# The order of the first two chunks written anew in a windowed-attention and feed-forward kernel

## The chip, the cores and the metric

The kernel runs on one core of a Trainium2 chip. The metric is the device time of one execution in microseconds (us); of several runs the median counts.

## What is computed

For 8 batches and 8 heads of 64 elements there are 512 local and 32 global tokens. A global token attends to all 544 tokens; a local one to the 32 global tokens and to the local tokens within 32 places. The heads are joined to rows of 512 elements, and each row then goes through a norm and a two-layer feed-forward network with a residual:

```python
s_ll = where(abs(pos[:, None] - pos[None, :]) <= 32, scale * q_l @ k_l.T, -1e9)
s_lg = scale * q_l @ k_g.T
out_l = sm(concat([s_lg, s_ll])) @ concat([v_g, v_l])
out_g = sm(scale * q_g @ k_all.T) @ v_all
x = join_heads(concat([out_g, out_l]))
xn = (x - mean(x)) / sqrt(var(x) + 1e-6) * g_ln
out = x + maximum(xn @ w_ch1, 0) @ w_ch2      # 512 -> 2048 -> 512
```

All of it is float32. A float32 product with enough precision is made of several products of high and low halves: a tile is split into a high part (a rounded copy) and a low part (what the rounding left).

## The kernel before, in words

The rows of x are worked in chunks of 512, one batch's local rows each, and a last one for the global rows. Chunk 0 needs its attention before its feed-forward part can start, and the weights have to be loaded, joined and split into halves while that part already runs. From chunk 1 on all weights lie ready in SBUF.

*Attention of chunk 0* comes in 8 units: 4 pairs of heads (0 to 3) times 2 halves of 256 rows. The numbers of units in this text, 0 to 7, are in the order of the program. A unit's steps, with engine and line of the kernel before:

- load of its tile `u` (queries, keys and values; SyncE, `dma`, L405); `score`, 32 small products per unit into two banks (TensorE, L542); `lowest`, four times, the mask with the row's minimum (VectorE, L554); `exp`, four times (ScalarE, L566)
- `turn`, four transposes `tp<-ident,p` (TensorE, L578); `turned`, their copy to SBUF (ScalarE, L583); `sums`, 32 small products `pv<-u,pt` (TensorE, L597); `total` (GpSimd, L609) and `inverse` (VectorE, L612) of the exponentials' sums; `scale`, the product of the two into x (VectorE, L616)
- the sums of a unit wait for the scaling of the unit before, and its `total` for the scaling three units before.

The *norm* of a half is `stats` (VectorE, L468, once for each pair of heads and 128 rows), `join` (L471), `widen` (L474), `root` (GpSimd, L478), `shift` (VectorE, L481), and `apply`, on ScalarE (L487) or VectorE (L493). Then `turn_x` transposes x (TensorE, L798) and `high_x` and `low_x` split it (ScalarE L812, VectorE L816).

The *weights* come in 16 pieces f of 128 hidden columns, each in two parts of 512 columns: load `raw<-in_wd` (L405), `bound`, a clamp (VectorE, L434), `size` and `third`, two conversions (ScalarE, L441 and L444), `place`, a merge of bits (VectorE, L447), `high` (ScalarE, L453) and `low` (VectorE, L456).

The *feed-forward part* takes for each f three groups of four products, high by high, high by low and low by high (`first`, L838, `ph<-xh,w`); `hh`, relu and rounding (ScalarE, L847); `hl`, the low half of the hidden tile (VectorE, L861); and four groups of three products (`second`, L873, `acc<-w,hh`). The `second` products of f stand behind the `first` ones of f+1.

Between them stand the *visits*: the attention of the next chunk's units, two units at a time, of tiles `u_e` (queries and keys) and `u_v` (values) that are loaded apart (L522 and L524). A visit makes the scores of the pair that comes next and the sums of the pair before (L542, L597). The loads for a later visit wait until the visit before has read the tiles.

Nothing is emitted where the code for it stands. `begin_plan` and its helpers build some 3000 numbered operations with `Plan.op`, each with an engine, the operations that it needs and a function that emits its instructions. `Plan.emit` then takes for each engine the operations in the order of the numbers in `ORDER` until that list is used up, and by key and reckoned time after that. `WARM` gives the number of warm-up products (L983, `none<-ident`, results used by nobody) that are put ahead of the TensorE operation with that number; where an operation isn't named there and the planner reckons with idle time ahead of it in the start, it puts in as many as fill that time:

```python
idle = max(free[e], AWAKE)
fill = int((t - idle - MARGIN) / spare) if t < FULL else 0
for _ in range(WARM.get(o.number, fill)):
    words += 2 * self.spare(idle)
```

SyncE issues the loads of the first chunks in the order of its list too, and waits at each until its tile is free. The lists cover the five engines to the end of the program; on TensorE the operations 17 to 191 are those of chunk 0's attention and norm, 625 to 793 the feed-forward part of chunk 0, with chunk 1's attention 422 to 621 in between.

Of the kernel before, what the change touches and what calls it, by code (L numbers as in the profile page):

```python
# [74 lines left out]
WARM = {19: 4, 28: 1, 53: 3, 102: 7, 170: 1, 625: 6}  # L75
# [11 lines left out]
        19 36 53 28 45 70 108 30 62 125 79 47 142 64 117 81 159 134 151 119 168 136 153 170 96-97 102-103  # L87
        184-186 191 625-627 422 630-632 635-641 644-650 653-658 445 659 662 433 663-664 451 665-668 671-677 474
        462 680-682 482 683-686 689-694 505 493 695 698 524 699-704 707-713 547 716-717 535 718-719 555 720-722
        725-731 734-740 743-749 752-758 781 761 784 787 762-764 790 765-768 1051-1053 793 1056-1058 1061-1067  # L90
        1070-1076 1079-1082 852 1083-1085 1088-1094 1097-1103 1106-1111 922 1112 1115-1121 1124-1130 1133-1139
        981 1142-1148 1151-1157 1160-1166 1169-1175 1178-1184 1187-1194 1537-1539 1279 1542-1544 1547-1553
        1556-1562 1565-1569 1338 1570-1571 1574-1580 1583-1589 1592-1597 1408 1598 1601-1607 1610-1616 1619-1625
        1467 1628-1634 1637-1643 1646-1652 1655-1661 1664-1670 1673-1680 2023-2025 1765 2028-2030 2033-2039
        2042-2048 2051-2055 1824 2056-2057 2060-2066 2069-2075 2078-2083 1894 2084 2087-2093 2096-2102 2105-2111
        1953 2114-2120 2123-2129 2132-2138 2141-2147 2150-2156 2159-2166 2509-2511 2251 2514-2516 2519-2525
        2528-2534 2537-2541 2310 2542-2543 2546-2552 2555-2561 2564-2569 2380 2570 2573-2579 2582-2588 2591-2597
        2439 2600-2606 2609-2615 2618-2624 2627-2633 2636-2642 2645-2652 2995-2997 2737 3000-3002 3005-3011
# [12 lines left out]
        403 617 568 592 619 397 408 618 521 414 593 399 742 594 569 411 595 620 596 413 570-571 622 572-573 751  # L111
        417 597 405 598 574 419 599-600 575 783 601 576 786 760 602 565 577-580 603-604 789 605 792 606-607 581
        591 775 779 773 1055 794 796 820 777 798 800 822 824 826 804 830 805 1060 806 831-834 807-811 835-837
        812 1069 838-839 813 840-841 814-816 851 842-844 817 803 818 850 829 819 1078 845 853 879 855 881 857
        883 909-910 859 885 913-914 862 915-916 863 1087 917 888-889 864 890 865 919 891 866 892 867 893 868 894
        869 895 870 896 1096 871 897 872 898 873 899 874 900 875 901 876 902 877 903 878 904 1207-1208 1105
        1209-1221 923 949 925 951 927 953 979-980 929 955 1222-1223 1114 933 932 959 958 934 960 935 961 936 962
        937 963 938 964 939 965 940 966 941 1123 967 942 968 943 969 944 970 945 971 946 972 947 973 948 974
        1224-1225 1132 1226-1238 1141 982 1008 984 1010 986 1038-1039 1012 988 1014 1042-1043 991 1044-1045 992
        1046 1017-1018 993 1019 994 1048 1020 995 1021 996 1022 997 1150 1023 998 1024 999 1025 1000 1026 1001  # L120
        1027 1002 1028 1003 1029 1004 1030 1005 1031 1239 1159 1240-1254 1168 1255-1270 1177 1006 1032 1007 1033
        1186 1272 1274 1276 1278 1199 1201 1203 1205 1541 1280 1306 1336-1337 1282 1308 1284 1310 1286 1312 1546
        1290-1291 1289 1315-1316 1292 1317 1293 1318 1294 1319 1295 1320 1296 1321 1297 1555 1322 1298 1323 1299
        1324 1300 1325 1301 1326 1302 1327 1303 1328 1304 1329 1305 1564 1330-1331 1339 1365 1395-1396 1341 1367
        1343 1369 1345 1371 1573 1399-1403 1348-1349 1374-1375 1350 1376 1405 1351 1377 1352 1378 1353 1582 1379
        1354 1380 1355 1381 1356 1382 1357 1383 1358 1384 1359 1385 1360 1386 1361 1591 1387 1362 1388 1363 1389
        1364 1390 1693-1703 1409 1435 1465-1466 1411 1437 1600 1413 1439 1415 1441 1704-1707 1419 1418 1445 1444
        1420 1446 1421 1447 1422 1448 1609 1423 1449 1424 1450 1425 1451 1426 1452 1427 1453 1428 1454 1429 1455
        1430 1618 1456 1431 1457 1432 1458 1433 1459 1434 1460 1708-1714 1627 1715-1724 1468 1494 1524-1525 1470
        1496 1472 1498 1474 1500 1528-1530 1636 1531-1532 1477-1478 1503-1504 1479 1505 1534 1480 1506 1481 1507  # L130
        1482 1508 1483 1509 1484 1510 1645 1485 1511 1486 1512 1487 1513 1488 1514 1489 1515 1490 1516 1491 1517
        1725-1726 1654 1727-1742 1663 1743-1756 1492 1672 1518 1493 1519 1758 1760 1762 1764 1685 1687 1689 1691
        2027 1766 1792 1822-1823 1768 1794 1770 1796 1772 1798 2032 1776-1777 1775 1801-1802 1778 1803 1779 1804
        1780 1805 1781 1806 1782 1807 1783 2041 1808 1784 1809 1785 1810 1786 1811 1787 1812 1788 1813 1789 1814
        1790 1815 1791 2050 1816-1817 1825 1851 1881-1882 1827 1853 1829 1855 1831 1857 2059 1885-1889 1834-1835
        1860-1861 1836 1862 1891 1837 1863 1838 1864 1839 2068 1865 1840 1866 1841 1867 1842 1868 1843 1869 1844
        1870 1845 1871 1846 1872 1847 2077 1873 1848 1874 1849 1875 1850 1876 2179-2189 1895 1921 1951-1952 1897
        1923 2086 1899 1925 1901 1927 2190-2193 1905 1904 1931 1930 1906 1932 1907 1933 1908 1934 2095 1909 1935
        1910 1936 1911 1937 1912 1938 1913 1939 1914 1940 1915 1941 1916 2104 1942 1917 1943 1918 1944 1919 1945
        1920 1946 2194-2200 2113 2201-2210 1954 1980 2010-2011 1956 1982 1958 1984 1960 1986 2014-2016 2122  # L140
        2017-2018 1963-1964 1989-1990 1965 1991 2020 1966 1992 1967 1993 1968 1994 1969 1995 1970 1996 2131 1971
        1997 1972 1998 1973 1999 1974 2000 1975 2001 1976 2002 1977 2003 2211-2212 2140 2213-2228 2149 2229-2242
        1978 2158 2004 1979 2005 2244 2246 2248 2250 2171 2173 2175 2177 2513 2252 2278 2308-2309 2254 2280 2256
        2282 2258 2284 2518 2262-2263 2261 2287-2288 2264 2289 2265 2290 2266 2291 2267 2292 2268 2293 2269 2527
        2294 2270 2295 2271 2296 2272 2297 2273 2298 2274 2299 2275 2300 2276 2301 2277 2536 2302-2303 2311 2337
        2367-2368 2313 2339 2315 2341 2317 2343 2545 2371-2375 2320-2321 2346-2347 2322 2348 2377 2323 2349 2324
        2350 2325 2554 2351 2326 2352 2327 2353 2328 2354 2329 2355 2330 2356 2331 2357 2332 2358 2333 2563 2359
        2334 2360 2335 2361 2336 2362 2665-2675 2381 2407 2437-2438 2383 2409 2572 2385 2411 2387 2413 2676-2679
        2391 2390 2417 2416 2392 2418 2393 2419 2394 2420 2581 2395 2421 2396 2422 2397 2423 2398 2424 2399 2425
        2400 2426 2401 2427 2402 2590 2428 2403 2429 2404 2430 2405 2431 2406 2432 2680-2686 2599 2687-2696 2440  # L150
# [1458 lines left out]
```

## Time and profile before

| | before |
|---|---|
| median of 3 runs | 882.84 us (881.62 to 883.41) |
| profiled execution | 883.14 us |
| its span in the trace | 881.3 us |
| TensorE products (PE) busy | 866.5 us, 98% of the span |
| VectorE (DVE) busy | 696.1 us, 79% |
| ScalarE (ACT) busy | 316.1 us, 36% |
| GpSimd (POOL) busy | 68.1 us, 8% |
| mean granted TensorE clock | 0.995 of full speed |

The table is of one execution. Busy time is the sum of an engine's instructions, and PEld, where it stands in a row, is TensorE's loading of weights, which runs beside its products. DMA is the mean busy share of the core's 16 DMA engines. A share over the whole span is a mean over stages with different limits: what bounds a stage is read from that stretch alone. "Idle before" behind a row of the order of time is the engine's idle time ahead of it, with the instruction that ended last before; the name is inferred.

### The profile page before, as it was taken

The numbers are of one execution on the slowest core, as the hardware profiler recorded it, in microseconds if no ns is written. First come the engines' busy times: TensorE is split into PE (matmuls) and PEld (weight loads), VectorE is DVE, ScalarE is ACT, GpSimd is POOL, SyncE is SP. The second block draws the span as 40 slices with busy tenths as digits, with TensorE's granted clock in tenths as the row PEclk, the third lists the DMA queues.
The fourth block names the chain that finished last, engine by engine and source line by source line (L and its number), as shares of the span: only waits on it lengthen the run. The fifth ranks groups of instructions, "written<-read, shape, count | busy, mean of one in ns | idle before, by whom it ended". The sixth has DMA issues, their size and how long they took to land.

```text
span 881.3 us, 21518 instructions
## 1 busy us (share of the span) xinstructions
PE 866.5 (98%) x8489; PEld 703.8 (80%) x8489; DVE 696.1 (79%) x2501; ACT 316.1 (36%) x895; POOL 68.1 (8%) x162
## 2 busy tenths in 40 slices
PE   7899999999999999999999999999999999999997
PEld 4588778888888888888888888888888788787897
DVE  4878688899778998799879997889879888787311
ACT  7788874223123223223223222223323222233211
POOL 4100000000000000000000000000000112222000
PEclk9999999999999999999999999999999999999999
DMA  9778835424124323324233403333331536355100
GB/s 345 295 245 279 283 100 184 157 82 152 43 87 134 115 87 129 105 80 152 81 106 126 152 0 128 104 104 128 128 105 48 204 130 221 121 195 198 65 21 24
DMA packets 42869, 119.88 MB, mean 136 GB/s; under 512 B 5136, under 2 KB 6160, under 8 KB 41744
## 3 DMA queue, kind: packets, MB, share of 16 engines
q1 hardware_dynamic: 42576, 118.25, 38.8%
q8 instruction: 66, 1.08, 0.5%
q14 instruction: 35, 0.29, 0.1%
q10 hardware_dynamic: 192, 0.26, 0.1%
HBM read 100.67 MB, written 17.83 MB: 134 GB/s over the span
## 4 chain that ended last, share of the span: by engine, by line
PE 93%; DVE 2%; DMA 2%; ACT 2%; issue 1%; POOL 1%; SPq 0%; ACTq 0%; POOLq 0%; DVEq 0%
PE ph L838 41%; PE acc L873 41%; PE sc L542 4%; PE pv L597 3%; PE pv L747 1%; PE sc L659 1%; DMA u_e<-in_eq 1%; ACT p L566 1%; DMA raw<-in_wd 1%; PE tp L578 1%; PE none L983 1%; PE t L798 1%; DVE w L456 0%; DVE tmp L447 0%; DVE p L554 0%
## 5 line engine op out<-in xcount | busy, mean ns | idle before, releaser
L873 PE MATMUL acc<-w,hh 128*128 128x512 f32 x1088 | 335.7, 390 | 0.0
L838 PE MATMUL ph<-xh,w 128*128 128x512 f32 (+1 forms) x1216 | 302.1, 375 | 1.1 <-DVE hl L861 1.0
L838 PEld LDWEIGHTS ph<-xh,w 128*128 128x128 f32 x1216 | 215.6, 188 | 43.8 <-DVE hl L861 1.7
L873 PEld LDWEIGHTS acc<-w,hh 128*128 128x128 f32 x1088 | 204.5, 188 | 41.4
L847 ACT ACTIVATE hh<-ph 128x512 fp32r<-128x512 f32 (+1 forms) x144 | 82.5, 573 | 415.2 <-PE ph L838 415.2
L589 DVE STREAM_TRANSPOSE pt<-p 32x128 f32<-32x128 f32 x768 | 207.2, 289 | 10.0 <-ACT p L566 1.6
L873 PE MATMUL acc<-w,hl 128*128 128x512 f32 x544 | 214.8, 395 | 0.0
L861 DVE SCALAR_TENSOR_TENSOR hl<-ph,hh 128x512 fp32r<-128x512 f32 (+1 forms) x125 | 82.1, 656 | 91.6 <-ACT hh L847 90.7
L838 PE MATMUL ph<-xl,w 128*128 128x512 f32 x512 | 137.8, 391 | 0.0
L566 ACT ACTIVATE p<-p,mn 128x128 f32<-128x128 f32 x256 | 99.9, 393 | 89.7 <-DVE mn L554 89.7
L806 DVE STREAM_TRANSPOSE tmp<-x 32x128 f32<-32x128 f32 x384 | 116.1, 302 | 5.8
L873 PEld LDWEIGHTS acc<-w,hl 128*128 128x128 f32 x544 | 102.2, 188 | 21.2
L838 PEld LDWEIGHTS ph<-xl,w 128*128 128x128 f32 x512 | 95.7, 188 | 20.3
L554 DVE CUSTOM_DVE_ANT_0 p<-sc,mask 128x128 f32<-128x128 f32 x256 | 60.7, 285 | 26.6 <-PE sc L542 19.5
L721 DVE STREAM_TRANSPOSE gpt<-gp 32x128 f32<-32x128 f32 x208 | 63.0, 303 | 3.4
L609 POOL TENSOR_SCALAR ri<-sm 128x4 f32<-128x4 f32 x64 | 15.6, 244 | 615.3 <-ACT p L566 613.8
L566 ACT ACTIVATION_READ_ACCUMULATOR p<-p,mn 128x1 f32 x256 | 48.4, 189 | 0.0
L542 PEld LDWEIGHTS sc<-u_e 64*32 64x32 f32 x1792 | 24.9, 105 | 10.3 <-issue 8.5
L542 PE MATMUL sc<-u_e 64*32 64x128 f32 x1792 | 32.4, 274 | 0.4 <-DMA u_e<-in_eq 0.4
L597 PE MATMUL pv<-u_v,pt 128*32 128x64 f32 x1792 | 31.1, 221 | 0.8 <-DVE mn L554 0.4
L597 PEld LDWEIGHTS pv<-u_v,pt 128*32 128x32 f32 x1792 | 26.5, 110 | 6.7 <-issue 6.1
L616 DVE TENSOR_TENSOR x<-pv,ri 128x256 f32<-128x256 f32 x64 | 24.9, 418 | 8.3 <-PE pv L597 4.8
(76 smaller groups left out, 500.8 us busy)
## 6 DMA issues: line engine op xcount, KB each, us to landing
u_v<-in_ev SPq DMA_DIRECT2D x56, 512.0 KB, 4.8
u_e<-in_eq SPq DMA_DIRECT2D x56, 336.0 KB, 6.5
raw<-in_wd SPq DMA_DIRECT2D x32, 512.0 KB, 7.1
gk<-in_gk SPq DMA_DIRECT2D x8, 1280.0 KB, 6.9
xs<-x SPq DMA_DIRECT2D x32, 256.0 KB, 6.6
ob<-xs SPq DMA_DIRECT2D x32, 256.0 KB, 6.1
out<-ob SPq DMA_DIRECT2D x32, 256.0 KB, 3.4
u<-in_ev SPq DMA_DIRECT2D x8, 512.0 KB, 9.7
```

The lines of the kernel that those rows point to most:

```text
L542: nc.tensor.matmul(sc[h][gp, qb * P:(qb + 1) * P], self.e[hd, w * WIN:(w + 1) * WIN], self.e[hd, k0 * WIN:(k0 + 4) * WIN], start=True, sto ...
L554: nc.vector.tensor_tensor_reduce(out=self.p[:, c], in0=self.sc[h][:, qb * P:(qb + 1) * P], in1=masks[self.at[2], qb], scale=-QSCALE, scala ...
L566: nc.scalar.activation(self.p[:, c], self.p[:, c], AF.Exp, bias=self.mn[:, c:c + 1], scale=-1.0, accum_out=self.sm[:, c:c + 1],)
L589: nc.vector.transpose(out=self.pt[rp, :, gp], in_=self.p[gp, :, rp])
L597: nc.tensor.matmul(pv[gp, qb * P + h * D:qb * P + h * D + D], self.pt[:, 2 * h + qb, gp], self.v[:, 4 * qb + g, h * D:(h + 1) * D], start= ...
L616: nc.vector.tensor_tensor(self.x[:, :, hp * P:(hp + 1) * P].rearrange("p q (h d) -> p q h d", h=2), self.pv[:, :256].rearrange("p (q h d) ...
L721: nc.vector.transpose(out=self.pt[rp, h, :n, ip], in_=p[ip, :, r])
L806: nc.vector.transpose(out=dst[rp, 2 * half:2 * half + 2, :, i], in_=src[ip, :, k:k + 2, r])
L838: nc.tensor.matmul(self.ph[f][:, :self.n], w[:, kt, :], xx[kt][:, :self.n], start=begins and kt == 0, stop=ends and kt == KT - 1,)
L847: nc.scalar.activation(hh[:, :self.n], self.ph[f][:, :self.n], AF.Relu)
L861: nc.vector.scalar_tensor_tensor(hl[:, :self.n], self.ph[f][:, :self.n], 0.0, f32(hh[:, :self.n]), ALU.max, ALU.subtract,)
L873: nc.tensor.matmul(self.acc[t], a[:, ts], w, start=(f == 0 and i == 0), stop=(f == NF - 1 and i == 2),)
```

## The change

The numbers in `ORDER` are put in another order for the first two chunks on all five engines, and two entries of `WARM` change. Each engine has the same operations as before. The lists agree from their 158th operation on for TensorE, from the 372nd on for VectorE, the 237th for ScalarE, the 28th for GpSimd and the 97th for SyncE. With the two lines that the lists grow by, every line of code behind them has a number that is higher by 2 (L578 becomes L580).

```diff
-WARM = {19: 4, 28: 1, 53: 3, 102: 7, 170: 1, 625: 6}
+WARM = {19: 4, 28: 1, 53: 3, 102: 9, 625: 6}
...
     "PE": """
-        19 36 53 28 45 70 108 30 62 125 79 47 142 64 117 81 159 134 151 119 168 136 153 170 96-97 102-103
+        19 36 53 28 45 70 108 30 62 125 79 47 142 64 117 159 134 81 151 119 168 136 153 96 170 97 102-103
...
     "POOL": """
-        17-18 31 48 65 82 120 137 154 92 171 181 443 431 460 472 491 503 545 533 564 520 621 590 802 828 861 887
+        17-18 31 48 65 82 120 137 154 171 92 181 431 443 472 503 460 491 533 545 520 621 802 828 564 590 887 861
```

Operations 96, 97, 102 and 103 are pairs of transposes of x, of the first 256 rows, and 170 is the sums of unit 7; 81 are the sums of unit 3 and 159 the scores of unit 7; 92 is the first half's root and 171 unit 7's total.

Three pieces of the order, first on TensorE from the transposes of unit 4 (before; with the change from right behind them) to those of x. Before:

```order
L578 MATMUL tp<-ident,p 128x128 x4
L597 MATMUL pv<-u,pt 32x64 x16
L542 MATMUL sc<-u 32x128 x16
L578 MATMUL tp<-ident,p 128x128 x8
L597 MATMUL pv<-u,pt 32x64 x16
L578 MATMUL tp<-ident,p 128x128 x4
L597 MATMUL pv<-u,pt 32x64 x48
L798 MATMUL t<-ident,x 128x128 x4
L983 LDWEIGHTS ident
L983 MATMUL none<-ident 128x512
```

and with the change:

```order
L544 MATMUL sc<-u 32x128 x16
L580 MATMUL tp<-ident,p 128x128 x4
L599 MATMUL pv<-u,pt 32x64 x16
L580 MATMUL tp<-ident,p 128x128 x4
L599 MATMUL pv<-u,pt 32x64 x16
L580 MATMUL tp<-ident,p 128x128 x4
L599 MATMUL pv<-u,pt 32x64 x32
L800 MATMUL t<-ident,x 128x128 x2
L985 LDWEIGHTS ident
L985 MATMUL none<-ident 128x512
L599 MATMUL pv<-u,pt 32x64 x16
L800 MATMUL t<-ident,x 128x128 x2
```

The scores of unit 7 (the sixteen L542 rows, L544 after) move ahead of the sums of unit 3, the sums of three units in a row come apart, and one pair of the transposes of x moves ahead of the last sums, with one warm-up product behind it. Seven warm-up products in a row ahead of the other transposes become nine.

VectorE between the scaling of unit 5 (first row) and that of unit 6 (last row), before:

```order
L616 TENSOR_TENSOR x<-pv,ri 128x2x128
L447 SCALAR_TENSOR_TENSOR tmp<-tmp,raw 128x512
L434 TENSOR_SCALAR tmp<-raw 128x512
L616 TENSOR_TENSOR x<-pv,ri 128x2x128
```

and with the change:

```order
L618 TENSOR_TENSOR x<-pv,ri 128x2x128
L470 BN_STATS st<-x 128x6
L483 SCALAR_TENSOR_TENSOR rs<-mv,rs 128x2
L495 TENSOR_SCALAR x<-x,mv,rs 128x512
L449 SCALAR_TENSOR_TENSOR tmp<-tmp,raw 128x512
L470 BN_STATS st<-x 128x6
L618 TENSOR_TENSOR x<-pv,ri 128x2x128
```

The clamp L434 goes from there to an earlier place, and two statistics (L470), the small shift (L483) and the application of the norm (L495) come in, which before stood ahead of these rows.

SyncE's issues in chunk 0, from the first load for the fourth visit (the one at 109 us in the rows below) on. Before:

```order
L405 DMA u_v<-in_ev 128x1024
L405 DMA raw<-in_wd 128x512 x3
L405 DMA u_e<-in_eq 128x672
L405 DMA xs<-x 128x512
L405 DMA raw<-in_wd 128x512 x2
L405 DMA u_e<-in_eq 128x672
L405 DMA u_v<-in_ev 128x1024
L405 DMA raw<-in_wd 128x512
L405 DMA xs<-x 128x512 x3
```

and with the change:

```order
L407 DMA u_v<-in_ev 128x1024
L407 DMA u_e<-in_eq 128x672
L407 DMA xs<-x 128x512
L407 DMA raw<-in_wd 128x512
L407 DMA u_e<-in_eq 128x672
L407 DMA xs<-x 128x512
L407 DMA u_v<-in_ev 128x1024
L407 DMA raw<-in_wd 128x512
L407 DMA xs<-x 128x512
```

The second `u_v`, the last load for that visit, stood behind five weight loads of these rows and now stands behind one; of the other four, one is now ahead of these rows and three come behind the `u_v`. Two stores to `xs`, the scratch for x in memory, are ahead of it instead of one.

## Rows read from the trace of the kernel before

**Rows 1.** Sums by stretch: stretch, length, busy (count), TensorE's granted clock, DMA share, GB/s
```profile
0.00:36.80 36.80, 28.74 (x581) 17.20 (x582) 23.33 (x122) 28.00 (x94) 11.17 (x52) 0.91 0.96 370
20.20:26.00 5.80, 5.80 (x107) 4.53 (x108) 2.99 (x18) 3.92 (x15) 1.19 (x3) 0.50 1.03 410
36.80:145.00 108.20, 105.93 (x1016) 86.44 (x1017) 85.86 (x249) 81.25 (x198) 4.95 (x12) 1.00 0.63 212
145.00:881.30 736.30, 731.83 (x6893) 600.20 (x6892) 586.95 (x2132) 206.84 (x604) 51.93 (x98) 1.00 0.33 113
```

**Rows 2.** TensorE in order of time, behind the start: start, length, instruction, [idle before]
```profile
41.20 1.19 PE L838 MATMUL ph<-xh,w 128*128 128x512 f32 x4 [0.33 <-DVE hl L861]
...
90.86 1.15 PE L542 MATMUL sc<-u_e 64*32 64x128 f32 x64 [0.42 <-DMA u_e<-in_eq]
...
93.32 0.42 PE L597 MATMUL pv<-u_v,pt 128*32 128x64 f32 x12 [0.41 <-issue]
...
109.36 1.10 PE L597 MATMUL pv<-u_v,pt 128*32 128x64 f32 x64 [0.42 <-DVE mn L554]
...
127.67 1.20 PE L838 MATMUL ph<-xh,w 128*128 128x512 f32 x4 [0.67 <-DVE hl L861]
```

**Rows 3.** The same view ahead of the first product
```profile
16.62 0.55 PE L578 MATMUL tp<-ident,p 128*128 128x128 f32 x3
20.20 0.47 PE L578 MATMUL tp<-ident,p 128*128 128x128 f32 x1 [3.02 <-ACT p L566]
...
28.93 0.66 PE L597 MATMUL pv<-u,pt 128*32 128x64 f32 x32 [0.61 <-ACT x L487]
...
30.01 2.98 PE L983 MATMUL none<-ident 128*128 128x512 bf16 x7
32.82 1.47 PE L798 MATMUL t<-ident,x 128*128 128x128 f32 x12
34.13 2.54 PE L983 MATMUL none<-ident 128*128 128x512 bf16 x6
36.82 1.16 PE L838 MATMUL ph<-xh,w 128*128 128x512 f32 x4
```

**Rows 4.** DMA queues from 13.4 to 20.3 us: packets, MB, share of engines
```profile
q8 instruction: 1, 0.02, 0.9%
```

**Rows 5.** VectorE in order of time, 9.0 to 10.7 us
```profile
9.30 0.29 DVE L554 CUSTOM_DVE_ANT_0 p<-sc,mask 128x128 f32<-128x128 f32 x1
...
10.43 0.18 DVE L612 RECIPROCAL ri<-ri 128x4 f32<-128x4 f32 x1 [0.36 <-POOL ri L609]
```

**Rows 6.** VectorE in order of time, 26.5 to 29.6 us
```profile
26.64 0.52 DVE L493 TENSOR_SCALAR x<-x,mv,rs 128x512 f32<-128x512 f32 x1
...
27.14 0.42 DVE L616 TENSOR_TENSOR x<-pv,ri 128x256 f32<-128x256 f32 x1
27.48 0.68 DVE L447 SCALAR_TENSOR_TENSOR tmp<-tmp,raw 128x512 int32<-128x512 int32 x1
28.08 0.42 DVE L434 TENSOR_SCALAR tmp<-raw 128x512 f32<-128x512 f32 x1
28.41 0.42 DVE L616 TENSOR_TENSOR x<-pv,ri 128x256 f32<-128x256 f32 x1
...
29.02 0.65 DVE L468 BATCH_NORM_STATS2 st<-x 128x6 f32<-128x128 f32 x3
```

**Rows 7.** The chain of waits, 80 to 94 and 115 to 128 us: start, length
```profile
82.84 7.88 DMA u_e<-in_eq
...
119.75 5.78 DMA raw<-in_wd
...
127.02 0.61 DVE hl L861
```

**Rows 8.** The tile u_v from 99 to 111 us: its load
```profile
L405 SPq DMA_DIRECT2D u_v<-in_ev x1: 328/328/328, 100.2 to 100.2; - x1
...
DMA to landing us min/median/max: 9.1/9.1/9.1
```

More of the change, by code (lines that the diff above doesn't have):

```diff
@@ new lines @@
+        677 474 680-681 482 682-686 689-692 493 505 693-695 524 698-704 707-708 547 709-711 535 712-713 716-717
+        555 718-722 725-731 734-740 743-749 752-758 781 784 761 787 762-765 790 766-768 1051-1053 793 1056-1058
+        1061-1067 1070-1076 1079-1082 852 1083-1085 1088-1094 1097-1103 1106-1111 922 1112 1115-1121 1124-1130
+        1133-1139 981 1142-1148 1151-1157 1160-1166 1169-1175 1178-1184 1187-1194 1537-1539 1279 1542-1544
+        1547-1553 1556-1562 1565-1569 1338 1570-1571 1574-1580 1583-1589 1592-1597 1408 1598 1601-1607 1610-1616
@@ new lines @@
+        1619-1625 1467 1628-1634 1637-1643 1646-1652 1655-1661 1664-1670 1673-1680 2023-2025 1765 2028-2030
+        2033-2039 2042-2048 2051-2055 1824 2056-2057 2060-2066 2069-2075 2078-2083 1894 2084 2087-2093 2096-2102
+        2105-2111 1953 2114-2120 2123-2129 2132-2138 2141-2147 2150-2156 2159-2166 2509-2511 2251 2514-2516
+        2519-2525 2528-2534 2537-2541 2310 2542-2543 2546-2552 2555-2561 2564-2569 2380 2570 2573-2579 2582-2588
+        2591-2597 2439 2600-2606 2609-2615 2618-2624 2627-2633 2636-2642 2645-2652 2995-2997 2737 3000-3002
@@ new lines @@
+        145 132 121 147 67 149 160 162 164 166 52 51 198 68-69 84-86 138 89-90 204 91 122 124 155 201 139 123 94
+        93 207 140 156 141 172 157-158 173-175 179 178 180 99 212 101 182-183 105 107 218 190 188 193 195 203
[6 rows of a table added]
+        391 618 397 567 399 568 619 742 620 403 408 622 592-593 414 594-595 569-570 596 411 751 417 571-572 597
+        413 573 598-599 574 405 600 575-576 419 760 601 577 783 602 786 789 603 578 604 579 792 580-581 605-607
+        777 775 773 820 1055 794 822 796 824 826 798 800 779 830-833 829 591 1060 804-806 834 807-809 835 810
@@ new lines @@
+        836-837 811 565 851 1069 812 850 838-839 813-815 840 816-817 803 841-842 818 843 819 1078 844-845 879
+        853 855 881 857 883 909-910 885 913 859 914-916 863 917 889 1087 862 888 864 890 865 919 891 866 892 867
+        893 868 894 869 895 870 896 1096 871 897 872 898 873 899 874 900 875 901 876 902 877 903 878 904
+        1207-1208 1105 1209-1221 923 949 925 951 927 953 979-980 929 955 1222-1223 1114 933 932 959 958 934 960
+        935 961 936 962 937 963 938 964 939 965 940 966 941 1123 967 942 968 943 969 944 970 945 971 946 972 947
@@ new lines @@
+        973 948 974 1224-1225 1132 1226-1238 1141 982 1008 984 1010 986 1038-1039 1012 988 1014 1042-1043 991
+        1044-1045 992 1046 1017-1018 993 1019 994 1048 1020 995 1021 996 1022 997 1150 1023 998 1024 999 1025
+        1000 1026 1001 1027 1002 1028 1003 1029 1004 1030 1005 1031 1239 1159 1240-1254 1168 1255-1270 1177 1006
+        1032 1007 1033 1186 1272 1274 1276 1278 1199 1201 1203 1205 1541 1280 1306 1336-1337 1282 1308 1284 1310
+        1286 1312 1546 1290-1291 1289 1315-1316 1292 1317 1293 1318 1294 1319 1295 1320 1296 1321 1297 1555 1322
@@ new lines @@
+        1298 1323 1299 1324 1300 1325 1301 1326 1302 1327 1303 1328 1304 1329 1305 1564 1330-1331 1339 1365
+        1395-1396 1341 1367 1343 1369 1345 1371 1573 1399-1403 1348-1349 1374-1375 1350 1376 1405 1351 1377 1352
+        1378 1353 1582 1379 1354 1380 1355 1381 1356 1382 1357 1383 1358 1384 1359 1385 1360 1386 1361 1591 1387
+        1362 1388 1363 1389 1364 1390 1693-1703 1409 1435 1465-1466 1411 1437 1600 1413 1439 1415 1441 1704-1707
+        1419 1418 1445 1444 1420 1446 1421 1447 1422 1448 1609 1423 1449 1424 1450 1425 1451 1426 1452 1427 1453
@@ new lines @@
+        1428 1454 1429 1455 1430 1618 1456 1431 1457 1432 1458 1433 1459 1434 1460 1708-1714 1627 1715-1724 1468
+        1494 1524-1525 1470 1496 1472 1498 1474 1500 1528-1530 1636 1531-1532 1477-1478 1503-1504 1479 1505 1534
+        1480 1506 1481 1507 1482 1508 1483 1509 1484 1510 1645 1485 1511 1486 1512 1487 1513 1488 1514 1489 1515
+        1490 1516 1491 1517 1725-1726 1654 1727-1742 1663 1743-1756 1492 1672 1518 1493 1519 1758 1760 1762 1764
+        1685 1687 1689 1691 2027 1766 1792 1822-1823 1768 1794 1770 1796 1772 1798 2032 1776-1777 1775 1801-1802
@@ new lines @@
+        1778 1803 1779 1804 1780 1805 1781 1806 1782 1807 1783 2041 1808 1784 1809 1785 1810 1786 1811 1787 1812
+        1788 1813 1789 1814 1790 1815 1791 2050 1816-1817 1825 1851 1881-1882 1827 1853 1829 1855 1831 1857 2059
+        1885-1889 1834-1835 1860-1861 1836 1862 1891 1837 1863 1838 1864 1839 2068 1865 1840 1866 1841 1867 1842
+        1868 1843 1869 1844 1870 1845 1871 1846 1872 1847 2077 1873 1848 1874 1849 1875 1850 1876 2179-2189 1895
+        1921 1951-1952 1897 1923 2086 1899 1925 1901 1927 2190-2193 1905 1904 1931 1930 1906 1932 1907 1933 1908
@@ new lines @@
+        1934 2095 1909 1935 1910 1936 1911 1937 1912 1938 1913 1939 1914 1940 1915 1941 1916 2104 1942 1917 1943
+        1918 1944 1919 1945 1920 1946 2194-2200 2113 2201-2210 1954 1980 2010-2011 1956 1982 1958 1984 1960 1986
+        2014-2016 2122 2017-2018 1963-1964 1989-1990 1965 1991 2020 1966 1992 1967 1993 1968 1994 1969 1995 1970
+        1996 2131 1971 1997 1972 1998 1973 1999 1974 2000 1975 2001 1976 2002 1977 2003 2211-2212 2140 2213-2228
+        2149 2229-2242 1978 2158 2004 1979 2005 2244 2246 2248 2250 2171 2173 2175 2177 2513 2252 2278 2308-2309
@@ new lines @@
+        2254 2280 2256 2282 2258 2284 2518 2262-2263 2261 2287-2288 2264 2289 2265 2290 2266 2291 2267 2292 2268
+        2293 2269 2527 2294 2270 2295 2271 2296 2272 2297 2273 2298 2274 2299 2275 2300 2276 2301 2277 2536
+        2302-2303 2311 2337 2367-2368 2313 2339 2315 2341 2317 2343 2545 2371-2375 2320-2321 2346-2347 2322 2348
+        2377 2323 2349 2324 2350 2325 2554 2351 2326 2352 2327 2353 2328 2354 2329 2355 2330 2356 2331 2357 2332
+        2358 2333 2563 2359 2334 2360 2335 2361 2336 2362 2665-2675 2381 2407 2437-2438 2383 2409 2572 2385 2411
@@ new lines @@
+        2387 2413 2676-2679 2391 2390 2417 2416 2392 2418 2393 2419 2394 2420 2581 2395 2421 2396 2422 2397 2423
+        2398 2424 2399 2425 2400 2426 2401 2427 2402 2590 2428 2403 2429 2404 2430 2405 2431 2406 2432 2680-2686
+        2599 2687-2696 2440 2466 2496-2497 2442 2468 2444 2470 2446 2472 2500-2503 2608 2504 2449-2450 2475-2476
+        2451 2477 2506 2452 2478 2453 2479 2454 2480 2455 2481 2456 2482 2617 2457 2483 2458 2484 2459 2485 2460
+        2486 2461 2487 2462 2488 2463 2489 2697-2698 2626 2699-2714 2635 2715-2728 2464 2490 2644 2465 2491 2730
@@ new lines @@
+        2732 2734 2736 2657 2659 2661 2663 2999 2738 2764 2794-2795 2740 2766 2742 2768 2744 2770 3004 2748-2749
+        2747 2773-2774 2750 2775 2751 2776 2752 2777 2753 2778 2754 2779 2755 3013 2780 2756 2781 2757 2782 2758
+        2783 2759 2784 2760 2785 2761 2786 2762 2787 2763 3022 2788-2789 2797 2823 2853-2854 2799 2825 2801 2827
+        2803 2829 3031 2857-2861 2806-2807 2832-2833 2808 2834 2863 2809 2835 2810 2836 2811 3040 2837 2812 2838
+        2813 2839 2814 2840 2815 2841 2816 2842 2817 2843 2818 2844 2819 3049 2845 2820 2846 2821 2847 2822 2848
@@ L162 @@
+        3151-3161 2867 2893 2923-2924 2869 2895 3058 2871 2897 2873 2899 3162-3165 2877 2876 2903 2902 2878 2904
+        2879 2905 2880 2906 3067 2881 2907 2882 2908 2883 2909 2884 2910 2885 2911 2886 2912 2887 2913 2888 3076
+        2914 2889 2915 2890 2916 2891
     """,
     "ACT": """
-        21 40 25 42 23 27 44 38 59 55 29 61 57 72 74 46 78 76 112 63 114 129 110 116 127 80 144 131 199-200 148
-        146 118 150 133 163 161 165 135 167 205 152 206 169 95 213 208 202 98 100 214 219 104 106 187 189 192
```

96 lines of the change are left out of this document (16 added, 80 removed), and 17 rows, old and new, of the table ORDER.

## The prediction

> **What bounds the kernel now.** I read first the sums over three stretches [rows 1]. Before the first feed-forward product TensorE is busy for 28.74 of 36.80 us, part of it with warm-up products that compute nothing. From 36.8 to 145 us, chunk 0 and the turn to chunk 1, it is busy for 105.93 of 108.20 us, and after 145 us the idle time of 4.47 us is that of the program's tail. The change rewrites the order up to there and little behind it. Its products are the same in number, so only two things can move the time: when the first product starts, and the 2.27 us that TensorE idles between it and 145 us.
>
> The second view is TensorE's own order of time, for those idle pieces [rows 2]. There are five: 0.33 us at 41.20 behind the first low half of the hidden tile, 0.42 us at 90.86 for a load of u_e, 0.41 us at 93.32 where the profile names nothing, 0.42 us at 109.36, and 0.67 us at 127.67, again behind a low half. They sum to 2.25 us, all there is to win behind the start.
>
> The third view is the same order ahead of the first product [rows 3]. One operation of four transposes runs three at 16.62, stands still for 3.02 us and runs the fourth at 20.20. The profile names ScalarE, but the same operation's other parts had what they needed; what arrives in this stretch is one packet of program code, 0.02 MB [rows 4], on DMA engines that are busy for 0.96 of the start [rows 1]. I read the pause as TensorE waiting for its program. [...] Then the units' sums and scalings go to and fro between TensorE and VectorE until the last sums at 28.93; seven warm-up products from 30.01, twelve transposes at 32.82, six warm-up products at 34.13, the first product at 36.82.
>
> [...]
>
> **The change, part by part.** *Start.* TensorE's order is the same up to the transposes that pause, so the code runs out at the same instruction. [...] Term: +0.2.
>
> Behind the pause the score of unit 7 now comes ahead of the sums of unit 3. The same four operations stand between the pause and the sums of unit 4, so those do not move. ScalarE takes two exponentials and the first weight tile's two conversions after the pause instead of before it; I cost this at nothing, since ScalarE had idle time there, at most 0.4 if that cover is too thin.
>
> The clear loss is VectorE's order between the scalings of units 5 and 6. The second waits for sums that wait for the first, and they start at 27.14 and 28.41 [rows 6]. Between them stand a merge of the weights and a clamp (0.33 us from its start to the next). Now the clamp is gone and two statistics (0.65/3 = 0.22 each), the small shift and the application of the norm (0.52 long, some 0.45 to the next start) come in. Balance: 2 x 0.22 + 0.45 - 0.33 = 0.56 us, later for the scaling of unit 6 and for the last sums behind it. Term: +0.6, bounds 0 (if the sums of unit 6 are late anyway) and 1.0 (GpSimd's root now also stands behind a total that waits for a scaling).
>
> One transpose pair is moved ahead of the last sums, into a wait: 2 x 1.47/12 = 0.25 us less behind them [rows 3]. Term: -0.25. Of the warm-up products nine instead of seven stand behind the second pair. One costs 2.98/7 = 0.43 us, and they run whether or not anything waits: before, they already ended at 32.99, just where the next transposes begin. Term: +0.85; bounds 0, if what the transposes need comes as much later, and 0.86. One more ahead of the last sums falls into the wait there: nothing. The six ahead of the first product stay.
>
> Sum for the start: 0.2 + 0.6 - 0.25 + 0.85 = +1.4 us, so the first product at about 38.2, between +0.2 and +2.2.
>
> *Behind the start.* The weights of chunk 0 are prepared by ScalarE and VectorE, which had time in hand there: 81.25 and 85.86 us busy of 108.20 [rows 1]. A start that is 1.4 us later gives them as much more, and I look only at the five pieces. The first (0.33) is the same three steps in a row and stays. The visit at 90.86 waited for u_e, which took 7.88 us from its issue [rows 7]; in SyncE's order the later of the pair's two u_e loads moves up by two places, and the visit itself moves up by one piece of products. Gone: -0.42. The 0.41 at 93.32 splits one visit's sums, 52 and 12, with nothing to wait for, and code is all that is left; the number of instructions ahead is almost the same, so it stays. At 109.36 the profile names VectorE, but the sums need a u_v that was issued at 100.2 and took 9.1 us [rows 8], that is until 109.3. It moves up past three weight loads and comes in time, although the visit moves up by two pieces. Gone: -0.42. At 127.67 the low half had waited on VectorE's queue behind the clamp of the last weights, whose load, issued at 119.75, landed after 5.78 us [rows 7]. In the new order that low half stands ahead of both clamps. Gone: -0.67. Sum: -1.51, bounds -2.25 (all five) and -0.4 (new waits in their place).
>
> Together +1.4 - 1.51 = -0.1 us. The profiled execution took 883.14 us, 0.30 above the median of 882.84; from the median I forecast **882.7 us**, no change.
>
> **Rivals.** *The pieces do not go, slower.* The loads of a visit are issued when the visit before it has read its tiles, so a TensorE that runs 1.4 us later also issues them 1.4 us later, and in SyncE's new order the last loads stand behind others that wait in this way. Then the start's loss stands alone: 882.84 + 1.4 = 884.2, or 885.0 at the upper end of the start. For it: the loads' 7.88 and 9.1 us are longer than the time between a visit and the next products. Against it: each of the two loads moves up in the queue by at least one transfer. It decides if u_v lands later than the visit's scores end. Chance 0.25.
>
> *The pause in the start shrinks, faster.* If the 3.02 us are a wait for ScalarE, or if the code arrives earlier because other loads stand in front of it, the stretch at half clock shrinks with it, but ScalarE's own work soon sets the end: from 20.2 to 26.0 us it is busy for 3.92 of 5.80 us [rows 1], so it has 1.9 us to give back. The start then comes to 1.4 - 1.9 = -0.5 us and the whole to -0.5 - 1.5 = -2.0: 880.8. Against it: three of the four transposes ran and nothing they shared was missing. Chance 0.12.
>
> *The warm-up products are covered, a little faster.* If what the transposes wait for is later by two warm-up products' time for other reasons, or the scaling does not slip, the start loses 0.2 and not 1.4: 881.5. Chance 0.15.
>
> **Numbers.** My forecast has 0.48. A measurement here tells about 0.2% from no change, 1.8 us, so the bounds are 881.1 and 884.6. Faster by more: the second rival, some of the third and the edge of the forecast, 0.12 + 0.06 + 0.05 = 0.23. Slower by more: two thirds of the first rival and an edge, 0.16 + 0.04 = 0.20. Within: 0.57. The range for 8 in 10 goes from 881.0 to 884.6: below it lies the lower part of the second rival, above it the first one's upper end.
>
> **What would show it.** In the new profile the last sums ahead of the transposes should start near 29.7, nine warm-up products should run until just before the next transposes, and the first product should start near 38.2. The pause after three transposes should be there, ending at 20.2 to 20.6, with the clock at 0.50 behind it. Of the five pieces, those at 41, and in the middle of one visit's sums, should be left, and TensorE's idle time up to its saturation should be 0.7 to 1.2 us. The forecast is wrong if the first product starts before 37.4 or after 39, if the pause is shorter by over 1 us, or if a new wait of over 0.5 us shows for a load in chunk 0.

## The result, and the profile after

The change makes the kernel slower. Its median is 890.88 us (890.50 to 891.49, 4 runs) beside 883.12 us for the kernel before in the same session (881.62 to 884.09, 4 runs); the ratio is 1.009 with a 95% interval of 1.0073 to 1.0108. The span of the profiled execution is 888.7 us, 7.4 us longer than before's 881.3.

First the sums by stretch of the changed kernel, cut where [rows 1] cut them, and then of the four stretches around the place where the time goes. The columns are those of [rows 1].

```profile
0.00:36.80 36.80, 28.86 (x579) 16.78 (x580) 19.91 (x113) 23.33 (x84) 11.05 (x52) 0.91 0.89 345
36.80:145.00 108.20, 102.12 (x989) 81.79 (x987) 82.47 (x240) 84.25 (x206) 3.67 (x10) 0.98 0.62 218
145.00:888.70 743.70, 739.25 (x6930) 606.09 (x6928) 593.94 (x2149) 208.24 (x607) 52.43 (x100) 1.00 0.32 112
...
105.00:109.00 4.00, 0.17 (x1) 0.18 (x2) 1.59 (x4) 0.74 (x2) 0.00 (x0) 1.00 0.73 292
109.00:113.50 4.50, 4.50 (x15) 3.60 (x16) 3.65 (x8) 3.77 (x7) 0.00 (x0) 0.62 0.43 101
```

Behind 145 us TensorE is idle for 4.45 us (4.47 before): nothing is lost there. Ahead of it there are two losses. In 36.8 to 145 us TensorE is busy for 102.12 us instead of 105.93, and nearly all of the difference lies between 105 and 109 us, where it does 0.17 us of work. In the 4.5 us behind that, the granted clock is 0.62 on the mean, so, as an estimate, 4.50 x (1 - 0.62) = 1.7 us more are lost. The other loss is the later start of the feed-forward part.

TensorE's own order of time, the view of [rows 2], shows both. These are all its idle pieces over 0.3 us behind the first product, with that product ahead of them:

```profile
39.49 1.15 PE L840 MATMUL ph<-xh,w 128*128 128x512 f32 x4
...
43.96 1.17 PE L840 MATMUL ph<-xh,w 128*128 128x512 f32 x4 [0.42 <-DVE hl L863]
...
94.35 1.10 PE L599 MATMUL pv<-u_v,pt 128*32 128x64 f32 x64 [0.73 <-DMA u_v<-in_ev]
...
108.83 1.61 PE L840 MATMUL ph<-xh,w 128*128 128x512 f32 x4 [4.49 <-DVE hl L863]
```

The first product starts at 39.49 instead of 36.82, 2.67 us later. Of the five pieces of [rows 2] the first is still there, the other four (0.42, 0.41, 0.42 and 0.67 us) are gone. In their place stand 0.73 us for a load of u_v and one wait of 4.49 us for the low half of a hidden tile.

What VectorE did meanwhile is in its own order of time:

```profile
99.77 0.43 DVE L436 TENSOR_SCALAR tmp<-raw 128x512 f32<-128x512 f32 x1
107.41 0.42 DVE L618 TENSOR_TENSOR x<-pv,ri 128x256 f32<-128x256 f32 x1 [7.21 <-DMA xs<-x]
107.75 0.42 DVE L436 TENSOR_SCALAR tmp<-raw 128x512 f32<-128x512 f32 x1
108.08 0.69 DVE L863 SCALAR_TENSOR_TENSOR hl<-ph,hh 128x512 fp32r<-128x512 f32 x1
```

VectorE stood still for 7.21 us at a scaling of the next chunk's attention, and the low half that TensorE needed was two places behind it on the same queue. The scaling waited for a store, `xs<-x`. It writes into the tile of x that the last store of chunk 0 (operation 177) still reads. SyncE's own view says when that store was issued:

```profile
85.46 11.56 SPq L407 DMA_DIRECT2D raw<-in_wd  x2
97.53 0.33 SPq L407 DMA_DIRECT2D u_v<-in_ev  x1
97.91 0.42 SPq L407 DMA_DIRECT2D u_e<-in_eq  x1
98.37 0.43 SPq L407 DMA_DIRECT2D xs<-x  x1
98.85 0.45 SPq L407 DMA_DIRECT2D raw<-in_wd  x1
99.34 0.83 SPq L407 DMA_DIRECT2D u_e<-in_eq  x1
100.21 0.77 SPq L407 DMA_DIRECT2D xs<-x  x1
```

The last of these rows is the store. Before, it was the 28th operation of SyncE's list and went out at 30.10 us:

```profile
30.10 0.33 SPq L405 DMA_DIRECT2D xs<-x  x1
```

Now it is the 65th: its data were ready some 70 us earlier, with the last scaling of chunk 0 at 31.66 us, but it stood behind weight loads and visit loads, among them one that SyncE could not issue until its tile was free (the first row covers 11.56 us from the first of two loads to the second). The chain of waits ties the pieces together:

```profile
100.21 7.11 DMA xs<-x
...
107.41 0.42 DVE x L618
107.83 0.34 DVE tmp L436
108.17 0.61 DVE hl L863
...
108.83 1.61 PE ph L840 x4
```

The start, beside [rows 3]:

```profile
17.56 0.55 PE L580 MATMUL tp<-ident,p 128*128 128x128 f32 x3
21.55 0.47 PE L580 MATMUL tp<-ident,p 128*128 128x128 f32 x1 [3.44 <-issue]
...
30.95 0.66 PE L599 MATMUL pv<-u,pt 128*32 128x64 f32 x32 [0.52 <-ACT pt L585]
31.53 0.44 PE L800 MATMUL t<-ident,x 128*128 128x128 f32 x2
31.81 3.84 PE L985 MATMUL none<-ident 128*128 128x512 bf16 x9
35.49 1.47 PE L800 MATMUL t<-ident,x 128*128 128x128 f32 x12
36.80 2.54 PE L985 MATMUL none<-ident 128*128 128x512 bf16 x6
```

The pause after three transposes ends 1.35 us later than before (21.55 against 20.20), the last sums start 2.02 us later (30.95 against 28.93), the twelve transposes 2.67 us later (35.49 against 32.82), and from there to the first product it is 4.00 us in both. So the start's loss has three parts: 1.35 by the end of the pause, 0.67 from there to the last sums, 0.65 from there to the transposes.

As an estimate the pieces add up: 2.67 us by the start, 4.49 + 0.73 us of new waits, 0.09 more at the first low half and 1.7 by the clock, less 1.92 us for the four pieces that are gone, make 7.8 us, where the span grew by 7.4.

### The profile page after: what moved, and what is told of

Same layout as the page of the kernel before. It is cut to its first block, busy times and chain, and to the rows that moved or that the text cites. A ratio compares the mean times of both kernels' runs of the same rounds, so it can differ in the third digit from the quotient of the medians.

```text
span 888.7 us, 21527 instructions
## 1 busy us (share of the span) xinstructions
PE 870.2 (98%) x8492; PEld 704.7 (79%) x8492; DVE 696.3 (78%) x2501; ACT 315.8 (36%) x895; POOL 67.1 (8%) x162
## 4 chain that ended last, share of the span: by engine, by line
PE 95%; ACT 1%; DMA 1%; DVE 1%; issue 1%; SPq 0%; DVEq 0%; ACTq 0%
PE ph L840 42%; PE acc L875 41%; PE sc L544 4%; PE pv L599 4%; PE pv L749 1%; PE sc L661 1%; DMA xs<-x 1%; PE tp L580 1%; ACT p L568 1%; DMA u<-in_eq 0%; PE t L800 0%; PE none L985 0%; SPq L407 0%; DVE p L556 0%; ACT xh L814 0%
## 5 line engine op out<-in xcount | busy, mean ns | idle before, releaser
L544 PEld LDWEIGHTS sc<-u_e 64*32 64x32 f32 x1792 | 24.9, 105 | 9.9 <-issue 8.8
L544 PE MATMUL sc<-u_e 64*32 64x128 f32 x1792 | 32.4, 274 | 0.0
```

Source lines behind the costliest of these rows:

```text
L544: nc.tensor.matmul(sc[h][gp, qb * P:(qb + 1) * P], self.e[hd, w * WIN:(w + 1) * WIN], self.e[hd, k0 * WIN:(k0 + 4) * WIN], start=True, sto ...
```

## Experiments

**The store, and its rival.** Theory A: the late store holds the tile, the scaling holds VectorE's queue, and so the low half is late. Rival B: the weights of piece 12, whose loads were moved behind those of a visit, are late by themselves, and the store is only the last name in the chain. Four kernels, first the store alone put back (a piece of SyncE's list):

```diff
-  252 449 88 176 253 266-267
+  252 449 88 176 177 253 266-267
...
-  365 552 177 549 378
+  365 552 549 378
```

> The changed kernel with one number moved: the last store of chunk 0's x (operation 177) goes back from the 65th place of SyncE's list to the place behind the other three stores. Theory A (the store holds the tile that the next chunk's fifth scaling writes, and VectorE's queue with the low half of the hidden tile stands behind that scaling): the wait of 4.49 us at 108.83 goes, with the 1.6 us that the lower clock behind it costs, so 884.5 to 885.5 instead of 890.9. Rival B (the weights of piece 12, whose loads now stand behind the loads of a visit, are late by themselves): a wait of 2 us or more stays there, over 888.

Measured: 883.29 us, ratio 0.9997 to before (0.9988 to 1.0006). The whole slowdown is gone from the median, although the first product still comes late, at 39.76 us. Its VectorE now runs the scaling at once and waits for the hidden tile instead of the hidden tile for it, and the one idle piece over 0.5 us on TensorE is another (0.98 us, at 95.81 in the same view of TensorE):

```profile
100.10 0.42 DVE L436 TENSOR_SCALAR tmp<-raw 128x512 f32<-128x512 f32 x1
100.44 0.42 DVE L618 TENSOR_TENSOR x<-pv,ri 128x256 f32<-128x256 f32 x1
100.77 0.42 DVE L436 TENSOR_SCALAR tmp<-raw 128x512 f32<-128x512 f32 x1
102.57 0.69 DVE L863 SCALAR_TENSOR_TENSOR hl<-ph,hh 128x512 fp32r<-128x512 f32 x1 [1.38 <-ACT hh L849]
```

No wait for the weights of piece 12 is left there, with their loads where the change put them: B falls. The median is 1.2 us under A's lower end. Its profiled execution, the slowest of its 12 runs with 884.74 us, has a span of 883.0, that is 5.7 us under the changed kernel's; by the rows above 4.49 + 1.7 = 6.2 were to be had. The rest of the difference between the medians lies outside what these two traces show. Beside before's span of 881.3 us its 883.0 is 1.7 us longer, near the estimate from the rows: 2.94 us of later start less 0.85 us, the idle pieces of [rows 2] being 2.25 us together and the two here (0.42 and 0.98) 1.40.

The same store moved alone, in the kernel before:

```diff
-  421 420 177 252-253
+  421 420 252-253
...
-  552 549 393
+  552 177 549 393
```

> The kernel before with the same store moved back to where the change has it, behind the last u_e of the fourth visit on SyncE's list. Theory A: the scaling at some 94 to 100 us waits for the store until about 107 us and a wait of 4 to 6 us opens on TensorE, 887.5 to 890. Rival B: 882.5 to 884, as before.

Measured: 886.80 us, ratio 1.0039 (1.0026 to 1.0053). One number on SyncE's list makes the kernel before slower, as A says and B does not, but by less than expected: the scaling again waits for the store, and TensorE for the scaling, for 2.13 us. VectorE and TensorE of that run:

```profile
108.69 0.42 DVE L616 TENSOR_TENSOR x<-pv,ri 128x256 f32<-128x256 f32 x1 [4.14 <-DMA xs<-x]
...
111.49 1.10 PE L597 MATMUL pv<-u_v,pt 128*32 128x64 f32 x64 [2.13 <-DVE x L616]
```

VectorE loses 4.14 us here and not 7.21: in before's order it has more to do ahead of that scaling. The price of a late store hangs on the rest of the lists.

The next two kernels split the order in time. On every engine the operations up to the first product come from one list and the rest from the other (a first part of 32 operations on TensorE, 84 on VectorE, 55 on ScalarE, 12 on GpSimd, 30 on SyncE; the store is in the first part):

```diff
-ORDER[e] = changed[e]
+ORDER[e] = [n for n in before[e] if n in first[e]] + [n for n in changed[e] if n not in first[e]]
```

> The order of before on all engines up to the first product of the feed-forward part, with before's warm-up products, and the changed order behind it; the store lies in the first part and is early. Theory A with a start that the new order makes later by 2.7 us: first product at 36.8, no wait of over 0.8 us behind it, 881.5 to 883. If the later start was that run's accident: the same as the run with the store moved alone, within 0.7 us.

> The changed order up to the first product of the feed-forward part with the changed warm-up products, and the order of before behind it; the store is early. Theory A: first product at 39.2 to 39.7, no wait of over 1 us behind it, 883.1 + 2.7 = 885.8, between 885 and 886.5. If the later start is regained behind it: 883 to 884.

Measured: 881.54 us, ratio 0.9980 (0.9970 to 0.9991), with before's first part and the changed rest; 886.06 us, ratio 1.0024 (1.0013 to 1.0035), with the changed first part and before's rest. The first beats both kernels. Its first product starts at 36.70, and 0.43 us at 41.20 is the only idle piece over 0.3 us that TensorE has between there and 145 us:

```profile
36.70 1.16 PE L840 MATMUL ph<-xh,w 128*128 128x512 f32 x4
...
41.20 1.16 PE L840 MATMUL ph<-xh,w 128*128 128x512 f32 x4 [0.43 <-DVE hl L863]
```

The second one's starts at 38.77, ahead of the 39.2 to 39.7 that were expected, and meets a wait of 2.11 us for u_e at 95.46, over the 1 us that was expected: that its time lies in A's range is luck. The later start, on the other hand, is no accident of one run: in the profiles with the changed first part the first product is at 39.49, 39.76 and 38.77, in those with before's at 36.82, 37.22 and 36.70.

**The pause in the start.** Of the start's 2.67 us, 1.35 were there when the pause ended, and no term of mine had that size. TensorE's order is the same until then, so the cause must be in what the other engines do ahead of it. Theory C: the changed loads make the code late. Rival D: VectorE's and ScalarE's order does. In the kernel before, SyncE's first 21 numbers in the changed order:

```diff
-  0 2 4 6 8 10 1 196 3 12 5 7 14 197 9 11 13 210 15-16 211
+  0 2 4 6 10 8 1 3 12 5 14 7 16 196 9 197 11 13 15 210-211
```

> The kernel before with SyncE's first 21 loads in the changed order (values of the units ahead of the first weights). Theory C (the code for TensorE takes longer to come because of what the changed list has in flight: 7.3 to 7.8 us from the packet before instead of 5.7 to 6.4): the pause ends at 21.3 to 21.9, first product 1 to 1.4 us later than before (37.8 to 38.4), 884.0 to 885. Rival D (the later start comes from VectorE's and ScalarE's order): the pause ends at 20.2 to 20.9 as before, first product 36.7 to 37.2, 882.5 to 883.8.

And in the kernel before, VectorE's first 50 and ScalarE's first 38 operations:

```diff
-ORDER["DVE"], ORDER["ACT"] = before["DVE"], before["ACT"]
+ORDER["DVE"] = [n for n in changed["DVE"] if n in before["DVE"][:50]] + before["DVE"][50:]
+ORDER["ACT"] = [n for n in changed["ACT"] if n in before["ACT"][:38]] + before["ACT"][38:]
```

> The kernel before with VectorE's first 50 and ScalarE's first 38 operations in the changed order; TensorE, SyncE and GpSimd as before. Theory C: the pause ends at 20.2 to 21.1, first product at most 0.4 us later than before, 882.5 to 884. Rival D: the pause ends at 21.3 to 21.9, first product at 37.8 to 38.4, 884.0 to 885.

Neither brought the pause's end to 21.3 us: 20.59 us with the loads, 20.41 with the two engines, where the profiles with before's whole start have 20.20 to 20.88. The first product is at 36.79 in the run with the loads (884.35 us, ratio 0.9997, 0.9984 to 1.0010). C and D both fall as single causes. The second kernel is slower for another reason, 889.07 us, ratio 1.0051 (1.0035 to 1.0066), with the first product at 42.15 us: behind the pause TensorE stops six times for 0.29 to 0.59 us between 23 and 31 us, and the granted clock is 0.50 from 28 to 37 us, where it was 1.00 before. That VectorE's order no longer fits TensorE's there is likely, and not tested. Its stretches from 20.2 to 28 and from 28 to 37 us:

```profile
20.20:28.00 7.80, 6.04 (x125) 4.32 (x129) 5.13 (x25) 5.68 (x20) 1.15 (x3) 0.62 1.03 409
28.00:37.00 9.00, 7.49 (x103) 3.90 (x96) 7.48 (x25) 5.80 (x11) 0.85 (x2) 0.50 0.85 304
```

and the same stretches of the kernel before:

```profile
20.20:28.00 7.80, 7.13 (x166) 5.56 (x170) 4.95 (x25) 5.92 (x19) 1.50 (x4) 0.63 1.03 410
28.00:37.00 9.00, 7.62 (x85) 3.86 (x74) 8.46 (x27) 7.47 (x16) 0.73 (x1) 1.00 1.02 400
```

TensorE had been idle for 1.76 us in the first stretch and not 0.67. That sum alone does not set the clock: the kernel before with the store late was idle for 1.73 us of the same first stretch, and in the second its twelve transposes took 1.47 us, as before's did at 1.00; in the run with the two engines' order they took 2.48 us, at 37.15.

So the question was turned round: on the changed kernel with the store early, the lists ahead of the pause were set back to before's order, one at a time and together. Theory F: the loads, together with the changed order elsewhere. Theory G: VectorE and ScalarE alone.

```diff
-ORDER["SP"] = changed["SP"]
+ORDER["SP"] = before["SP"][:21] + changed["SP"][21:]
```

> The changed kernel with the store early (as in the first experiment) and SyncE's first 21 loads in the order of before. Theory F (the changed loads make the code late only together with the changed order of the other engines): the pause ends at 20.2 to 20.9 instead of 21.5 to 21.9, and the first product comes at 38.4 to 38.9. Theory G (VectorE's and ScalarE's changed order alone brings the pause's end later on the changed TensorE order): the pause ends at 21.3 to 21.9, first product 39.4 to 39.9.

```diff
-ORDER["DVE"], ORDER["ACT"] = changed["DVE"], changed["ACT"]
+ORDER["DVE"] = before["DVE"][:18] + changed["DVE"][18:]
+ORDER["ACT"] = before["ACT"][:26] + changed["ACT"][26:]
```

> The changed kernel with the store early and the first 18 operations of VectorE and 26 of ScalarE, those ahead of the pause, in the order of before; SyncE's loads as changed. Theory F: the pause ends at 21.3 to 21.9 or up to 0.5 us earlier. Theory G: it ends at 20.2 to 20.9, first product 38.4 to 38.9.

Both of these at once:

> Both of these at once: SyncE's first 21, VectorE's first 18 and ScalarE's first 26 operations in the order of before, the rest as in the changed kernel with the store early. By F and by G the pause ends at 20.2 to 20.9 and the first product comes at 38.4 to 38.9: what is left of the later start is the order behind the pause and the warm-up products, 1.3 us. If the pause still ends at 21.3 or later, neither list makes it.

The pause's end and the first product, from TensorE's order of time in each run, the run with the loads set back first, then the two engines, then all three:

```profile
20.90 0.47 PE L580 MATMUL tp<-ident,p 128*128 128x128 f32 x1 [2.73 <-issue]
...
38.98 1.17 PE L840 MATMUL ph<-xh,w 128*128 128x512 f32 x4
```

```profile
21.18 0.33 PE L580 MATMUL tp<-ident,p 128*128 128x128 f32 x1 [3.85 <-issue]
...
38.47 1.17 PE L840 MATMUL ph<-xh,w 128*128 128x512 f32 x4
```

```profile
20.49 0.47 PE L580 MATMUL tp<-ident,p 128*128 128x128 f32 x1 [2.59 <-issue]
...
38.41 1.16 PE L840 MATMUL ph<-xh,w 128*128 128x512 f32 x4
```

All three lists set back bring the pause's end to 20.49, into the range of before's start (20.20 to 20.88); the loads alone bring it to 20.90, to that range's edge, and the two engines alone to 21.18, against 21.48 to 21.85 in the three profiles with the changed first part. G fails in both runs. F's ranges for the pause hold, at their edges; its first product with the loads set back was to come by 38.9 and came at 38.98. The run with the two engines set back tests VectorE only in part: its first 18 operations end at 12.9 us, the pause begins at 17.3, and between them it runs the changed order. Times: 883.32 us (ratio 0.9991, 0.9977 to 1.0005), 883.02 (0.9989, 0.9974 to 1.0004) and 882.90 (0.9983, 0.9969 to 0.9996).

The traces say more than the pause's end, because the packet of program code is in them, the one of [rows 4], and another one ahead of it (starts read in slices of 0.05 us):

| kernel | packet ahead | packet | between | pause ends |
|---|---|---|---|---|
| before | 11.40 | 17.80 | 6.40 | 20.20 |
| changed | 11.80 | 19.15 | 7.35 | 21.55 |
| before, changed loads | 11.35 | 18.10 | 6.75 | 20.59 |
| before, changed VectorE and ScalarE | 11.45 | 18.20 | 6.75 | 20.41 |
| changed, store early, loads set back | 12.10 | 18.55 | 6.45 | 20.90 |
| changed, store early, two engines set back | 11.35 | 18.70 | 7.35 | 21.18 |
| changed, store early, all three set back | 11.85 | 18.05 | 6.20 | 20.49 |

In all 13 profiles the fourth transpose runs 2.2 to 2.5 us behind the packet's start; the view does not name the packet's engine, and that it is TensorE's is read from this distance. [rows 4] has one of two packets of code in that stretch: a smaller one, 0.01 MB on q14, starts at 19.8 us before and at 21.0 in the changed kernel, 0.4 and 0.5 us ahead of the pause's end. Which of the two TensorE waited for is not shown. Of the 1.35 us, 0.40 are there when the packet ahead starts and 0.95 lie between the two packets. The first is within the scatter: with before's whole start the packet ahead comes at 11.40 to 12.30 us. The second is not: the time between is 6.10 to 6.45 us with before's whole start, and 7.25 to 7.70 in the four profiles with the changed loads and all or most of the other changed lists. Setting the loads back takes it to 6.45, setting the two engines back leaves it at 7.35. So the loads make the larger share, but on the kernel before they reach only 6.75. What they need beside them is open, and these are single profiles.

**The warm-up products.** Two kernels put a price on them. Nine instead of seven in the kernel before, and five instead of seven in the version with before's first part and the changed rest:

```diff
-WARM = {19: 4, 28: 1, 53: 3, 102: 7, 170: 1, 625: 6}
+WARM = {19: 4, 28: 1, 53: 3, 102: 9, 170: 1, 625: 6}
```

> The kernel before with nine instead of seven warm-up products ahead of the other transposes of x. Where they are a pure cost, as the prediction's term has it: first product 0.86 us later (37.6 to 38.1), 883.5 to 884.5. Where what the transposes need would come later anyway: first product 36.8 to 37.3, no change.

> The kernel with before's order up to the first product and the changed order behind it, with five instead of seven warm-up products ahead of the other transposes. Where they are a pure cost: first product 0.86 us earlier (35.8 to 36.1), about 880.7. Where the transposes wait for the low halves (ended at 32.39 before) and the norm of the second half (32.84): at most 0.4 us earlier, 881.1 to 881.6, with an idle piece in their place.

With nine it takes 4.16 us from the first transposes (29.25) to the others (33.41), where before it takes 3.30 (29.52 to 32.82): the two cost their full 0.86 us, and the first product is at 37.41, a little ahead of the 37.6 that were expected, since its first transposes start 0.27 us earlier than before's. The time, 884.05 us, ratio 0.9999 (0.9985 to 1.0012), does not resolve it. With five it takes 7.01 us from the first transposes (30.00) to the first product (37.01) instead of 7.30: 0.29 us won of 0.86, because the transposes then wait for the low halves:

```profile
30.49 2.11 PE L985 MATMUL none<-ident 128*128 128x512 bf16 x5
32.92 1.57 PE L800 MATMUL t<-ident,x 128*128 128x128 f32 x12 [0.32 <-DVE xl L818]
```

Its ratio, 0.9976 (0.9964 to 0.9987; median 881.76 us), cannot be told from the 0.9980 with seven.

## Why the prediction was wrong

I forecast 882.7 us and no change, in a range of 881.0 to 884.6; it took 890.88. The steps, one by one.

*The wait that was not priced.* The step that failed is "I look only at the five pieces", with its bound of -0.4 us for "new waits in their place". I followed each moved load forward to its visit, but a store is issued by the same queue, and of the stores I looked at none. Operation 177 went from the 28th to the 65th place on SyncE's list, and asking who waits for it would have led to the scaling that writes the same tile, and from there down VectorE's queue to the low half. That chain is worth 4.49 us of idle TensorE and some 1.7 us of lower clock, and moving the one number back took the whole slowdown away. Two of the forecast's own signs of being wrong came true: a first product after 39 us, and a wait of over 0.5 us for a load. The slower rival named a queue in which loads stand behind others that wait. That queue is where it happened, but its price was the start's loss alone, 1.4 us, and its condition, a u_v that lands late, is the piece of 0.73 us and not the one of 4.49.

*The gains behind the start.* Right in kind, and in size as far as the runs can tell. I had -1.51: the waits of 0.42, 0.42 and 0.67 us went as argued, the 0.33 at the first low half stayed, and the 0.41 us that I took for program code and left standing is also gone (a packet of code on q8 starts at 90.86 us in the kernel before, 2.46 us ahead of the product behind that wait). Without the late store and the later start the sum is seen alone: in the kernel with before's first part and the changed rest, the median is 2.1 us under that of before in its session (881.54 against 883.63), and the interval of its ratio, 0.8 to 2.7 us, holds the 1.51. In its trace TensorE is idle for 0.55 us from the first product to 145 us, where before it was 2.27.

*The start.* Forecast +1.4 us, bounds +0.2 and +2.2; measured +2.67. Two of its parts were right: VectorE's order between the scalings and what lies around it, +0.6, measured 0.67 from the pause to the last sums (0.59 of it between the two scalings, which start at 28.57 and 30.43 and no longer at 27.14 and 28.41); the two warm-up products less the moved pair of transposes, 0.85 - 0.25 = 0.60, measured 0.65. The failed term is the +0.2 for what the new order does ahead of the pause, to VectorE's minimum of [rows 5] among others: it was my estimate, and no run shows it. In its place the pause ended 1.35 us later: the three transposes started 0.94 us later, nearly five times the term, and the pause itself grew from 3.02 to 3.44 us, which had no bound at all. Told by the code packets, 0.40 us are there when the packet ahead starts, within the scatter; the 0.95 us more between the two packets, for which the changed loads are the larger share, had no term.

*The reading of the pause.* It held, as a reading of distances in time. In all 13 profiles TensorE stops behind the same three transposes, for 2.59 to 3.85 us, and where the profile of before named ScalarE that of the changed kernel names nothing. A wait for ScalarE is ruled out by its own order of time: the four exponentials that these transposes read had ended by 16.53 us before and by 16.89 in the changed kernel, ahead of the three transposes. And the pause ends a near constant time, 2.2 to 2.5 us, behind the start of the code packet. The rival in which the new order closes the pause found nothing to support it.

*The third rival*, warm-up products that are covered, fell in the kernel before: two more cost 0.86 us. Two fewer show that they stand close to a wait: only 0.29 us came back.

## What to carry to other kernels

When an order of issue is rewritten, follow the stores as well as the loads: here a store that left at 100.21 us instead of 30.10 held its source tile, and the next writer of that tile held VectorE, with all that was queued behind it, for 7.21 us. A rearranged list is worth splitting in time before it is judged; here the rest of the new order is a gain of 0.2% (ratio 0.9980, 0.9970 to 0.9991) that its start and one late store hid. And a small edit to one list is read on the queue of the engine that waits, not on the engine that idles: TensorE's 4.49 us name a low half, and it takes VectorE's own view, or the chain of waits, to name the store.

## What the runs showed that was not expected

Idle time of TensorE cost more than itself: behind its 4.49 us without work the granted clock was 0.62 on the mean for 4.5 us. The length of the idle time is not the whole of it. In the kernel before, the clock was 0.50 behind the pause of 3.02 us in the start, where TensorE then worked without a stop from 20.20 to 27.0 us, and it was back at 26 us (0.99 from 26.0 to 26.5). In the run with VectorE's and ScalarE's order alone the pause was 2.80 us long, TensorE stopped six times between 23 and 31 us, and the clock was still 0.50 from 28 to 37 us. That these short stops kept it down is read from two traces and not tested.
